# Spacing attention work and gate splits in the last loop of a fused attention and SwiGLU kernel, with a second accumulator bank

## The chip, the core and the metric

The kernel runs on one core of a Trainium2 chip. A core has five engines that run side by side, each with its own in-order stream of instructions: TensorE (matrix products, "PE" in the profile, with its weight loads as "PEld"), VectorE ("DVE"), ScalarE ("ACT"), GpSimd ("POOL") and SyncE ("SP", which here starts DMA transfers). [...]TensorE writes its products into PSUM, a memory of eight banks of 128 partitions by 512 fp32 values. The metric is device time in microseconds, less is better. The kernel before takes 292.16 us, the median of three runs (292.1 to 293.44).

## The reference

Two blocks follow each other. The first is a linear attention on polynomial sketches, the second a SwiGLU layer on its output.

```python
def phi(x):
    a = einsum('rd,bhsd->bhsr', S1, x)          # r = 8
    b = einsum('rd,bhsd->bhsr', S2, x)
    return einsum('bhsi,bhsj->bhsij', a, b).reshape(..., 64)
q_p, k_p = phi(q), phi(k)                       # 4 batches, 4 heads, 1088 tokens, 32 wide
kv  = einsum('bhsf,bhsd->bhfd', k_p, v)
z   = sum(k_p, axis=2)
num = einsum('bhsf,bhfd->bhsd', q_p, kv)
den = einsum('bhsf,bhf->bhs', q_p, z)[..., None] + 1e-06
x   = (num / den) laid out as 4352 tokens x 128
g   = x @ w_gate                                # 128 x 1536
out = (g * sigmoid(g) * (x @ w_val)) @ w_out    # 1536 x 128
```

All inputs and outputs are fp32.

## The kernel before

**Tiling.** The 4352 tokens are cut into twelve blocks, three for each of the four batches, of 384, 384 and 320 tokens. The hidden width of 1536 is twelve chunks of 128. A *unit* `(i, j)` computes chunk `j` of the hidden layer for block `i`: a gate product, a value product, Silu of the gate, and their product, which lands in a slot of `hbuf`. A *down* product (`down`, L962) multiplies one such slot by the rows of `w_out` of that chunk and adds it, in PSUM, to the block's output; after the twelfth, `store` (L993) transposes the accumulator on VectorE (L997) and sends it out. Before the last loop the kernel runs attention for batch 0 and most of the first three blocks' units; the last loop (L1237) runs the other nine blocks, `line`, 108 units counted by `y`, block by block, with attention of batches 2 and 3 threaded through.

**Two forms of a product.** An fp32 product costs TensorE two passes of 384 columns for each weight tile. In `cut_unit` (L887) a product is instead made from parts of its operands: tokens and weights are each split into a high and a low part that TensorE takes in one pass (`x1`, `x0`, `w1`, `wb`) and one correcting combination of both (`xd`, `wd`). Three one-pass products then stand for one fp32 product: `wd` by `xd` (L896), `w1` by `x1` (L904) and `wb` by `x0` (L905). ScalarE evicts the first with a scale (L900), and VectorE adds the sum of the other two to it (L906, the *combine*). `cut_unit` always treats the value product like this. With `both` it treats the gate so too, and the eviction and the combine are twice as wide; without `both` the gate is one fp32 product (L898), and Silu (L912) reads it from PSUM. GpSimd makes the product of gate and value (L917). With `both`, the Silu and the last product of a unit are put off (`ending`) until the next unit has put its first products and its eviction into the streams (`finish`, L927).

**The order of downs.** A unit that is done is appended to `todo`. After every unit of the last loop, up to two downs are taken while more than five are left (L1248), or more than six when the next one would be the first of its block. In that last case a unit passes without a down, and the next takes two.

**PSUM.** Banks are numbered 0 to 7: `g0` = 0, `g1` = 1, `g2` = 2, `acc` = 3, `a` = 4 and 5, `b` = 6 and 7. In the last loop `bank()` hands out the bank whose last hand-out lies furthest back (`used`), leaving out the ones that are held; `pair()` does so among the pairs that start at 0, 4 and 6. Bank 3 is held for the down products of whichever block is under way.

**Attention in the last loop.** `attentions` (L603) is a generator. Each `yield` ends a *part*: a few instructions, mostly VectorE's (a product that makes features, L365, of up to 768 columns; a transpose, L750; the denominator, L735 to L741, five dependent instructions in one part). `parts_of` runs the next part; it stops in front of a yield of `"pe"`, which marks a *group* of TensorE work that is run at the units listed in `GROUPS`. For batch 2 these groups are: kv and the sums (L698), with the sketches of the next keys; the query sketches. For batch 3: the numerators of batch 2 (L758) with kv; the query sketches. The fifth is the numerators of batch 3. After kv, `fold` (L585) and `spread_out` (L711) have VectorE read kv's bank: four short instructions in a row, ending with the transpose at L716. The last of the first three, at L596, makes the third sketch that the query sketches need.

**The order in the streams.** Nothing is reordered by a scheduler: the kernel is written with a manual schedule, and each engine's instructions stand in the order of the Python calls. The order above is thus the order on every engine, and waits follow from data and from banks and buffers that are used again.

The lines of the last loop that matter: L1226 sets `GROUPS` to `(5, 7, 22, 24, 40)` and `GATES` to 18; L1245 uses both products in parts from `GATES` on; L1250 runs one part after every unit up to 21, and after every second from then on.

Of the kernel before, what the change touches and what calls it, by code (L numbers as in the profile page):

```python
# [19 lines left out]
def kernel(  # L20
# [30 lines left out]
    B, H, S, Dh = q.shape  # L51
# [38 lines left out]
    used = {i: 0 for i in range(8)}  # L90
# [4 lines left out]
    def touch(*which):  # L95
        for i in which:
            clock[0] += 1
            used[i] = clock[0]

    def hold(*tags):  # L100
        for t in tags:
            held.update((place[t], place[t] + 1) if t in "ab" else (place[t],))

    def release(*tags):
        for t in tags:
            banks = (place[t], place[t] + 1) if t in "ab" else (place[t],)
            held.difference_update(banks)
            touch(*banks)

    def bank(tag=None):  # L110

        if tag is not None:
            i = place[tag]
        elif oldest[0]:
            i = min((i for i in used if i not in held), key=used.get)
        else:
            i = place[free_banks[turn[0] % len(free_banks)]]
            turn[0] += 1
        touch(i)
        return PS[:, i, :]  # L120
# [7 lines left out]
    def wide(tag):  # L128
        i = place[tag]
        touch(i, i + 1)  # L130
        return PS[:, i : i + 2, :]
# [423 lines left out]
    def turn_keys(b):  # L555

        for c in kpieces:
            turn_k(*c)
            if c[1] == NC and b + 1 < B:
                load_k(b + 1)  # L560
            yield

    def turn_queries(b):

        for x0, x1 in ((0, 4 * kpieces[0][1]), (4 * kpieces[0][1], 4 * NC)):
            nc.vector.transpose(out=qT[:, x0:x1, :], in_=qld[:, x0:x1, :])
            if x1 == 4 * NC and b + 1 < B:
                load_q(b + 1)
            yield
# [33 lines left out]
    def attentions():  # L603

        yield from turn_keys(1)
        yield from turn_queries(1)
        hold("a")
        kp = wide("a")  # L610
        for i, c in enumerate(kpieces):
            key_products(kp[:, i, :], *c)
        ka = apool.tile([P, NC * H, R], FP32, tag="kas", name="kas")

        def sketch(ps, i):
            c0, c1 = kpieces[i]
            return ps[:, i, 0 : 64 * (c1 - c0)].rearrange("p (x t r) -> p x t r", t=2, r=R)

        for i, (c0, c1) in enumerate(kpieces):
            nc.scalar.copy(ka[:, H * c0 : H * c1, :], sketch(kp, i)[:, :, 0, :])  # L620
        phk = apool.tile([P, NC, H, R, R], FP32, tag="phk", name="phk")
        for n, (i, c0, c1) in enumerate(((0, 0, 3), (0, 3, 5), (1, 5, 7), (1, 7, 9))):
            first = H * (c0 - kpieces[i][0])
            kb = sketch(kp, i)[:, first : first + H * (c1 - c0), 1, :]
            key_features(phk, (ka[:, H * c0 : H * c1, :], kb), c0, c1)
            if n == 3:
                release("a")
            if n % 3 != 1:
                yield
        zs, sums = feature_sums(phk)  # L630
        for f in sums:
            f()
        yield from turn_keys(2)
        kvz = wide("a")
        values(kvz[:, 0, :], phk, zs)
        kab, kcopies = sketched(wide("b"), key_products, 2, "kab2")
        fold(kvz[:, 0, :])
        spread = spread_out(1, kvz[:, 0, :])
        hold("a", "b")
        yield  # L640
        qab, copies = sketched(wide("a"), query_sketches, 3, "qab")
        run_copies(copies, 2)
        yield
        run_copies(kcopies, 2)
        release("a", "b")
        for n, _ in enumerate(query_step(1, qab)):
            if n % 2 == 0:
                yield
        yield
        yield  # L650
        numerators(1, spread)
        yield "first"

        phk = apool.tile([P, NC, H, R, R], FP32, tag="phk", name="phk")
        yield from features(phk, kab)
        zs, sums = feature_sums(phk)
        for f in sums:
            f()
        yield from turn_keys(3)
        yield from turn_queries(2)  # L660
        for b in (2, 3):
            yield "pe"
            if b == 3:
                numerators(2, spread)
            hold("a")
            kv = bank()
            release("a")
            values(kv, phk, zs)
            if b == 2:
                kab, copies = sketched(wide("a"), key_products, 2, "kab2")  # L670
                run_copies(copies, 2)
            fold(kv)
            spread = spread_out(b, kv)
            yield
            yield "pe"
            qab, copies = sketched(wide("b"), query_sketches, 3, "qab")
            run_copies(copies, 2)
            yield
            if b == 2:
                yield from turn_queries(3)  # L680
                phk = hbuf[:, NH - 6 :, :].rearrange("p s (n h i j) -> p (s n) h i j", h=1, i=R, j=R)
                phk = phk.rearrange("p (c h) o i j -> p c (h o) i j", h=H)
                yield from features(phk, kab)
                zs, sums = feature_sums(phk)
            yield from beside(query_step(b, qab), sums)
        yield "pe"
        numerators(3, spread)
        yield
# [13 lines left out]
    def values(kv, phk, zs):  # L702

        key_values(kv[:, 0:F], phk, 0, NC)
        for h in range(H):
            nc.tensor.matmul(
                kv[32 * h : 32 * h + 32, F : 2 * F], ones[:], zs[:, F * h : F * h + F],
                start=True, stop=True,
            )

    def spread_out(b, kv):  # L711

        spread = apool.tile([P, H, F], FP32, tag="spread", name="spread")
        nc.vector.transpose(  # L716
            out=spread[:, 0, :].rearrange("p (g d) -> p g d", g=2),
            in_=kv[:, 0:F].rearrange("p (g f) -> p g f", g=2),
        )
        for s in range(1, H):  # L720
            m = P - 32 * s
            nc.sync.dma_start(out=spread[0:m, s, :], in_=spread[P - m : P, 0, :])
            nc.sync.dma_start(out=spread[m:P, s, :], in_=spread[0 : P - m, 0, :])
        if b + 1 < B:
            load_v(b + 1, [nc.sync] * 4)
        return spread
# [64 lines left out]
    acc = {}  # L791
    todo = []
# [134 lines left out]
    def finish():  # L927
        while ending:
            ending.pop(0)()
# [28 lines left out]
    def catch_up():  # L958
        o, sg = lates.pop(0)
        nc.gpsimd.tensor_tensor(out=o, in0=o, in1=sg, op=ALU.mult)  # L960

    def down():  # L962

        i, j = todo.pop(0)
        n = SPLIT if i == LAST else blocks[i][1]
        if j == 0:
            acc[i] = bank("g1" if i == 1 else "acc")
        nc.tensor.matmul(  # L968
            acc[i][:, 0:n],
            wo[:, j, :],  # L970
            hidden[i, j][:, 0:n],
            start=(j == 0),
            stop=(j == NCH - 1),
        )
        if i != LAST:
            hidden.pop((i, j))
            slots.append(slot_of[i, j])
        if j == NCH - 1:
            store(i, n)
# [136 lines left out]
    def parts_of(n):  # L1116

        for _ in range(n):
            if ahead[0] not in ("pe", "end"):
                ahead[0] = next(att, "end")  # L1120
                begun[0] |= ahead[0] == "first"

    def group():
        while ahead[0] != "pe":
            ahead[0] = next(att)
        ahead[0] = next(att, "end")
# [94 lines left out]

    line = [3 * b + k for b in range(1, B) for k in ((0, 2, 1) if b == B - 1 else range(3))]
    END = len(line) * NCH
    GROUPS, GATES = (5, 7, 22, 24, 40), 18  # L1226

    token_steps = {}
    for m, i in enumerate(line[1:], 1):
# [7 lines left out]
    for y in range(END):  # L1237
        i, j = line[y // NCH], y % NCH
        if y in GROUPS:
            group()  # L1240
        if y == END - 1:
            finish()
            unit(i, j)
        else:
            cut_unit(i, j, both=y >= GATES)  # L1245
        for _ in range(2):

            if len(todo) > min(5 + (todo[0][1] == 0), END - y + 1):  # L1248
                down()
        parts_of(y < 22 or y % 2 == 0)  # L1250
        if y == 0:
            gate_rows = cut_weights(wg, lows, nc.vector)
        for n, row in enumerate(gate_rows):
            if y >= (0, 2, 6, 6)[n]:
                take(row, 1)
        for gen in token_steps.get(y, ()):
            next(gen, None)
# [8 lines left out]
    b, x0 = divmod(t0 // 32, NX)  # L1266
# [34 lines left out]
```

## Time and profile before

| what | value |
|---|---|
| median time | 292.16 us |
| profiled span | 290.1 us |
| TensorE busy | 280.2 us, 97% |
| VectorE busy | 207.7 us, 72% |
| ScalarE busy | 173.7 us, 60% |
| GpSimd busy | 161.8 us, 56% |
| last loop starts (y = 0) | 92.6 us |
| combine L906, 384 / 640 / 768 columns | 0.534 / 0.820 / 0.955 us |
| eviction L900, 384 / 640 / 768 columns | 0.490 / 0.704 / 0.811 us |
| feature product L365 of 768 columns, queries | 1.239 us |
| transpose L750 of 768 columns | 0.965 us |
| transpose of an output block L997, 384 / 320 columns | 0.567 / 0.504 us |

How to read it: the page gives for each engine the time in which it executed something, and for each group of instructions a mean time. Matmuls are pipelined: the recorded time of one overlaps that of the next, so an fp32 product, which is recorded as two matmuls of some 0.49 us, is best priced by the distance between starts. The weight loads in front of the products show better where TensorE stood still: the timeline gives, in square brackets, how long the engine was idle before an instruction and what released it. The chain of waits goes back from the last instruction to what each had to wait for; its rows give start, length and work.

### The profile page before, as it was taken

How to read it: one execution, taken by the hardware profiler on the slowest of the kernel's cores; microseconds unless marked ns; L12 is line 12 of the kernel's file. 1: busy time of each engine (PE TensorE's matmuls, PEld its weight loads, DVE VectorE, ACT ScalarE, POOL GpSimd, SP SyncE). 2: the span in 40 equal slices, each digit the busy share in tenths (PEclk: the TensorE clock that was granted, in tenths of full speed). 3: DMA queues.
4: the chain of work that ended last, by engine and by line, in shares of the span. 5: the costliest groups of instructions: out<-in, count | busy, mean ns of one | idle time of the engine just before them, and what ended most of it. 6: DMA issues, size and time to landing. Idle time of an engine off the chain costs nothing.

```text
span 290.1 us, 6038 instructions
## 1 busy us (share of the span) xinstructions
PE 280.2 (97%) x2311; PEld 211.5 (73%) x2311; DVE 207.7 (72%) x337; ACT 173.7 (60%) x347; POOL 161.8 (56%) x183
## 2 busy tenths in 40 slices
PE   7899999999999989989989999999999999999995
PEld 7545566656656857756868878888888988889884
DVE  4997988874677959999489956756656567575741
ACT  3567565732403757545567776677687776777760
POOL 3316322379302984689438655675665666755750
PEclk9999999999999999999999999999999999999999
DMA  6564292302501302000001001001001010010101
GB/s 194 162 208 111 64 311 73 124 32 84 115 15 17 99 17 79 0 14 14 15 3 30 1 2 23 0 0 31 0 0 27 2 24 1 2 27 1 21 4 27
DMA packets 26141, 14.32 MB, mean 49 GB/s; under 512 B 19840, under 2 KB 24192, under 8 KB 26112
## 3 DMA queue, kind: packets, MB, share of 16 engines
q1 hardware_dynamic: 25456, 13.84, 18.3%
q8 instruction: 18, 0.29, 0.4%
q10 hardware_dynamic: 656, 0.10, 0.2%
q14 instruction: 11, 0.09, 0.1%
HBM read 11.41 MB, written 2.23 MB: 47 GB/s over the span
## 4 chain that ended last, share of the span: by engine, by line
PE 86%; DVE 8%; issue 2%; DMA 1%; ACT 1%; SPq 0%; DVEq 0%; ACTq 0%
PE PS L968 27%; PE PS L939 15%; PE PS L904 11%; PE PS L896 11%; PE PS L905 10%; PE PS L898 3%; PE PS L768 2%; PE PS L330 2%; DVE sum L906 1%; DMA kld<-in_k_dram 1%; PE PS L342 1%; PE PS L376 1%; DVE phk L365 1%; PE PS L983 1%; DVE kT L315 1%
## 5 line engine op out<-in xcount | busy, mean ns | idle before, releaser
L917 POOL TENSOR_TENSOR hbuf<-sg,sum 128x384 f32<-128x384 f32 (+1 forms) x107 | 108.9, 1022 | 62.2 <-ACT sg L912 53.4
L906 DVE SCALAR_TENSOR_TENSOR sum<-PS,sum 128x768 f32<-128x768 f32 (+2 forms) x107 | 89.5, 839 | 49.4 <-ACT sum L900 44.6
L900 ACT ACTIVATE sum<-PS 128x768 f32<-128x768 f32 (+2 forms) x107 | 77.2, 721 | 47.0 <-PE PS L896 40.3
L968 PE MATMUL PS<-hbuf,wo 128*128 128x384 f32 (+2 forms) x288 | 103.0, 459 | 0.0
L968 PEld LDWEIGHTS PS<-hbuf,wo 128*128 128x128 f32 x288 | 52.0, 189 | 10.3 <-issue 0.4
L896 PE MATMUL PS<-xd,gphq 128*128 128x384 f32 (+1 forms) x89 | 49.1, 551 | 2.3 <-DVE sum L906 2.3
L912 ACT ACTIVATE sg<-sum 128x384 f32<-128x384 f32 (+1 forms) x89 | 44.0, 495 | 3.5 <-DVE sum L906 3.2
L904 PE MATMUL PS<-x,w 128*128 128x384 f32 (+1 forms) x107 | 40.4, 377 | 0.1
L896 PE MATMUL PS<-xd,wd 128*128 128x384 f32 (+1 forms) x107 | 38.1, 356 | 0.2 <-DVE xd L872 0.2
L905 PE MATMUL PS<-x,wb 128*128 128x384 f32 (+1 forms) x107 | 35.1, 328 | 0.0
L904 PE MATMUL PS<-x,graw 128*128 128x384 f32 (+1 forms) x89 | 29.9, 336 | 0.2 <-ACT xT L785 0.2
L939 PE MATMUL PS<-xT,wg 128*128 128x384 f32 (+1 forms) x74 | 29.5, 480 | 0.0
L939 PE MATMUL PS<-xT,wv 128*128 128x384 f32 (+1 forms) x74 | 28.8, 471 | 0.2 <-DVE wv L276 0.2
L905 PE MATMUL PS<-x,graw 128*128 128x384 f32 (+1 forms) x89 | 29.0, 326 | 0.0
L896 PEld LDWEIGHTS PS<-xd,wd 128*128 128x128 f32 x107 | 20.3, 190 | 10.0 <-issue 0.7
L943 ACT ACTIVATE sg<-PS 128x384 f32<-128x384 f32 (+1 forms) x31 | 14.3, 466 | 21.4 <-PE PS L939 19.8
L896 PEld LDWEIGHTS PS<-xd,gphq 128*128 128x128 f32 x89 | 16.8, 189 | 13.1 <-DVE sum L906 4.9
L954 DVE TENSOR_TENSOR hbuf<-sg,PS 128x384 f32<-128x384 f32 (+1 forms) x31 | 16.2, 524 | 10.5 <-PE PS L939 10.1
L904 PEld LDWEIGHTS PS<-x,w 128*128 128x128 f32 x107 | 20.1, 188 | 2.8 <-DVE sum L906 0.4
L905 PEld LDWEIGHTS PS<-x,wb 128*128 128x128 f32 x107 | 20.1, 188 | 2.4
L939 PEld LDWEIGHTS PS<-xT,wv 128*128 128x128 f32 x74 | 13.8, 190 | 9.2 <-DVE hbuf L954 0.9
L939 PEld LDWEIGHTS PS<-xT,wg 128*128 128x128 f32 x74 | 13.3, 190 | 9.3 <-issue 1.2
(131 smaller groups left out, 346.6 us busy)
## 6 DMA issues: line engine op xcount, KB each, us to landing
kld<-in_k_dram SPq DMA_DIRECT2D x4, 544.0 KB, 3.9
vld<-in_v_dram SPq DMA_DIRECT2D x12, 144.0 KB, 4.6
qld<-in_q_dram SPq DMA_DIRECT2D x3, 544.0 KB, 3.4
raw<-in_moe_w_out_dram SPq DMA_DIRECT2D x4, 384.0 KB, 4.0
out_dram<-o SPq DMA_DIRECT2D x28, 48.0 KB, 1.8
raw<-in_moe_w_gate_dram SPq DMA_DIRECT2D x3, 384.0 KB, 3.2
raw<-in_moe_w_val_dram SPq DMA_DIRECT2D x3, 384.0 KB, 3.5
out_dram<-o SPq DMA_DIRECT2D x16, 40.0 KB, 1.7
```

Source lines behind the costliest of these rows:

```text
L896: nc.tensor.matmul(ds[:, k], wd, xd, start=True, stop=True)
L898: nc.tensor.matmul(g, wg[:, j, :], xT[:, t0 : t0 + n], start=True, stop=True)
L900: nc.scalar.activation(sums, ds, AF.Copy, scale=-1.0 / BETA)
L904: nc.tensor.matmul(ps[:, k], w1, x1, start=True, stop=False)
L905: nc.tensor.matmul(ps[:, k], wb, x0, start=False, stop=True)
L906: nc.vector.scalar_tensor_tensor(out=sums, in0=ps, scalar=1.0 + 1.0 / BETA, in1=sums, op0=ALU.mult, op1=ALU.add)
L912: nc.scalar.activation(sg, sums[:, 0] if both else g, AF.Silu)
L917: nc.gpsimd.tensor_tensor(out=hj[:, 0:n], in0=sg, in1=sums[:, len(ws) - 1], op=ALU.mult)
L939: nc.tensor.matmul(o[:, 0:n], w[:, j, :], xT[:, t0 : t0 + n], start=True, stop=True)
L943: nc.scalar.activation(sg[:, 0:n], g[:, 0:n], AF.Silu)
L954: nc.vector.tensor_tensor(out=hj[:, 0:n], in0=sg[:, 0:n], in1=u[:, 0:n], op=ALU.mult)
L968: nc.tensor.matmul(acc[i][:, 0:n], wo[:, j, :], hidden[i, j][:, 0:n], start=(j == 0), stop=(j == NCH - 1),)
```

## The change

There are four edits, all in the order of work of the last loop and in the choice of banks.

1. *Attention's parts are spaced differently.* One part after every unit up to y = 7, then after two units in three (not those where `y % 3 == 2`), and from y = 26 on after one unit in three. The groups of batch 3 move from 22, 24 and 40 to 26, 28 and 52.
2. *Gates in parts start otherwise.* They were in parts from y = 18 on. Now they are in parts from y = 26 on, and before that in every third unit from y = 11 (11, 14, 17, 20, 23), the ones that have no attention part.
3. *Two accumulator banks in turn.* The third, fifth, seventh and ninth block of the loop collect their downs in bank 2, the others in bank 3; bank 2 is held from y = 26 on. The rule that a down which starts a block waits for one more unit now holds for the second block of the loop only, so for the others each unit keeps its down.
4. *The bank of kv counts as used again* after the VectorE instructions that read it have been put into the stream, so that it isn't the next to be handed out.

The aim of the first two is to keep VectorE's load beside TensorE's even, that of the third to take away the dependence of a block's first down on the transpose of the block before it, and that of the fourth to keep TensorE off a bank that is still being read.

```diff
             kv = bank()
+            kv_bank = [max(used, key=used.get)]
             release("a")
             values(kv, phk, zs)
...
             fold(kv)
             spread = spread_out(b, kv)
+            touch(*kv_bank)
             yield
...
+    line = [3 * b + k for b in range(1, B) for k in ((0, 2, 1) if b == B - 1 else range(3))]
...
         if j == 0:
-            acc[i] = bank("g1" if i == 1 else "acc")
+            acc[i] = bank("g1" if i == 1 else "g2" if i in line[2::2] else "acc")
...
-    line = [3 * b + k for b in range(1, B) for k in ((0, 2, 1) if b == B - 1 else range(3))]
     END = len(line) * NCH
-    GROUPS, GATES = (5, 7, 22, 24, 40), 18
+    GROUPS, GATES = (5, 7, 26, 28, 52), 26
...
         if y in GROUPS:
             group()
+        if y == GATES:
+            hold("g2")
         if y == END - 1:
             finish()
             unit(i, j)
         else:
-            cut_unit(i, j, both=y >= GATES)
+            cut_unit(i, j, both=y >= GATES or (y > 10 and y % 3 == 2))
         for _ in range(2):
 
-            if len(todo) > min(5 + (todo[0][1] == 0), END - y + 1):
+            if len(todo) > min(5 + (todo[0] == (line[1], 0)), END - y + 1):
                 down()
-        parts_of(y < 22 or y % 2 == 0)
+        parts_of(y < 8 or (y % 3 != 2 if y < GATES else y % 3 == 0))
```

## The prediction

> **What bounds the kernel now.** I read the engine shares first, then the windows of each stage, then what the weight loads wait for, and last the timeline around each wait.
>
> ```profile
> PE 280.2 (97%) x2311; PEld 211.5 (73%) x2311; DVE 207.7 (72%) x337; ACT 173.7 (60%) x347; POOL 161.8 (56%) x183
> ...
> PE 86%; DVE 8%; issue 2%; DMA 1%; ACT 1%; SPq 0%; DVEq 0%; ACTq 0%
> ```
>
> TensorE is the bound, but a busy PE hides its waits, so I look at windows:
>
> ```profile
> 109.00:123.00 14.00, 14.00 (x56) 9.88 (x54) 13.64 (x21) 8.80 (x19) 8.37 (x7) 1.00 0.14 40
> 123.00:136.00 13.00, 11.73 (x49) 8.03 (x47) 13.00 (x17) 6.54 (x13) 11.99 (x12) 1.00 0.10 16
> ...
> 176.00:278.00 102.00, 102.00 (x514) 87.01 (x513) 64.52 (x76) 75.20 (x133) 65.12 (x68) 1.00 0.07 12
> ```
>
> The columns are length, then busy time of PE, PEld, DVE, ACT and POOL. From 109 to 136 us VectorE is full (13.64 of 14.00, then 13.00 of 13.00): attention work for batches 2 and 3 beside the combines of L906. From 176 us on it has a third of its time free and TensorE runs without rest. Number the 108 units of the last loop y = 0 to 107: y=6 starts at 102.3, y=15 at 122.0, y=18 at 127.2, y=24 at 144.7, y=44 at 179.1 us. The weight loads' waits, first for 92 to 180, then for 176 to 280 us (total, times, longest):
>
> ```profile
> PEld PS L896 <- DVE sum L906: 5.4, 8, 1.7
> PEld PS L898 <- DVE spread L716: 1.3, 1, 1.3
> ```
>
> ```profile
> PEld PS L904 <- ACT sum L900: 1.4, 6, 0.2
> ```
>
> And in the timeline one example of each:
>
> ```profile
> 103.57 0.30 PEld L898 LDWEIGHTS PS<-xT,wg 128*128 128x128 f32 x2 [1.26 <-DVE spread L716]
> 130.16 0.19 PEld L896 LDWEIGHTS PS<-xd,gphq 128*128 128x128 f32 x1 [1.49 <-DVE sum L906]
> 150.62 0.19 PEld L896 LDWEIGHTS PS<-xd,gphq 128*128 128x128 f32 x1 [1.70 <-DVE sum L906]
> 217.16 0.19 PEld L904 LDWEIGHTS PS<-x,graw 128*128 128x128 f32 x1 [0.23 <-ACT sum L900]
> ```
>
> So there are four kinds of lost time: a gate product put into the bank of kv that VectorE still reads (103.57); VectorE behind at y=15 to 20 (130.16); one long chain of the denominator on VectorE (150.62); and a block boundary, where a unit has no down product to fill the wait for ScalarE (217.16).
>
> Two unit prices come from the chain of waits. With the gate as one fp32 product, from down pair to down pair:
>
> ```profile
> 118.19 0.65 PE PS L968 x2
> ...
> 120.00 0.65 PE PS L968 x2
> ```
>
> 1.81 us. With both products in parts:
>
> ```profile
> 192.49 0.65 PE PS L968 x2
> ...
> 194.19 0.64 PE PS L968 x2
> ```
>
> 1.70 us. Gates in parts save TensorE 0.11 to 0.12 us a unit (about 0.10 at 320 columns), but the combine grows from 0.54 to 0.95 us on VectorE and the eviction L900 from 0.49 to 0.81 us on ScalarE.
>
> **What the Trainium skill says.** *Perfetto Trace Analysis*, section "Identifying the Most-Contended Engine": the matmul busy share is no good measure, weight-load busy is better. The trace agrees: 123 to 136 us shows PE at 90% but weight loads at only 8.03 of 13 us, against 87.01 of 102 later. The same page, "Optimization Strategy": a gap that repeats can mean too few buffers; here it is 0.2 us, six times, once per block, with one accumulator bank. *SBUF — State Buffer*, "SBUF: two separate sides": VectorE with two SBUF inputs and GpSimd take a shared port pair as an exclusive lock. The trace fits: the feature product L365 of 768 takes 0.94 us at 123.98 and 1.68 us at 130.03, with GpSimd busy 11.99 of 13 us. So VectorE's sums below are a little low. *PSUM — Partial Sum Buffer*, "PSUM bank collisions raise a hardware error": banks must be guarded whole; that is why a product waits for any reader of its bank, as at 103.57.
>
> **Part by part.**
>
> *touch(kv_bank) and down threshold (y=5, 6).* In the built order of before, the gate of y=6 goes to bank 0, where kv is, and waits for the last of fold, reduce, s123, spread. After, kv counts as freshly used, that gate goes to bank 4, whose reader (the kab copy) ended at 101.5. One down also moves from y=6 into y=5. The query sketches L330 still need s123, ready at 103.36, and the combine of y=5, at 103.96; TensorE gets to them at about 104.8 to 105.0 in place of 106.06. VectorE stood idle until 109.22 here, so it moves along. **-1.1** (bounds -0.3 and -1.26).
>
> *Parts spread, gates later (y=8 to 25).* I summed VectorE's instructions per unit in the built order, by row means (combine 0.54 or 0.95, feature product 1.25, transpose 0.96, denominator chain 2.7, xd 0.6, o 0.57), against TensorE's 1.81 or 1.70. Before: from y=8 VectorE's arrears grow to 2 us at y=11, 3 at y=13, 4 at y=15, and stay at 3 to 4 until the group at y=22. TensorE's two-unit cushion is about 2 us, so it stalls: y=15 to 20 take 12.37 us for 9.8 us of products, 2.55 us lost. After: three units cost TensorE 2 x 1.81 + 1.70 = 5.3 us, VectorE 2 x 0.54 + 0.95 + two parts of 1.1 = 4.2 us. The sum of arrears starts at 1.4 (y=10), is 0 at y=14 and never over 1.3. The new wait: a unit with both products finishes its Silu only in the next unit, so it has no down behind it, and ScalarE's next evictions queue behind a Silu that waits for VectorE's combine. Following y=17 to 22 through by these durations, TensorE loses 0.1 to 0.3. I leave 0.35 in all. **-2.2** (bounds -2.5 and -0.5).
>
> *Gate count.* Parts before: y=18 to 106, 89 units; after: 11, 14, 17, 20, 23 and 26 to 106, 86 units. Three units more with an fp32 gate at 0.10 to 0.12. **+0.3**, on the path.
>
> *The group of y=22, now 26.* Before, the numerators waited 0.55 + 0.37 us for VectorE and ScalarE in arrears. After, VectorE is level there. **-0.4** (0 to -0.9).
>
> *First gates in parts at 26, and batch 3's denominator.* This chain lies on VectorE thus before:
>
> ```profile
> 146.82 1.04 DVE L735 TENSOR_TENSOR dot<-qab 128x288 f32<-128x288 f32 x1
> 147.90 0.45 DVE L738 TENSOR_REDUCE den<-dot 128x36 f32<-128x288 f32 x1
> 148.39 0.54 DVE L739 TENSOR_SCALAR den<-den 128x36 f32<-128x36 f32 x1
> 148.96 0.38 DVE L740 RECIPROCAL den<-den 128x36 f32<-128x36 f32 x1
> 149.37 0.46 DVE L741 TENSOR_TENSOR qab<-qab,den 128x288 f32<-128x288 f32 x1
> 149.75 1.55 DVE L906 SCALAR_TENSOR_TENSOR sum<-PS,sum 128x640 f32<-128x640 f32 x2
> ```
>
> The combine behind it held TensorE 1.70 us; y=24 to 29 lose 1.2 us net. The change does not break the chain, it only moves it to y=31 and 32, where the downs are 320 wide (0.54 for 0.65), so the cushion is 0.3 us thinner: about 1.5 us again, and 0.2 when the next feature product comes. At y=26 there is no down, and y=27's pair contains kv's bank 1 (fold to spread, about 1 us): 0.4. **+0.6** (0 to +1.3). Later parts, one in three units: 3 x 0.95 + 1.1 = 4.0 of 5.1 us, no stall.
>
> *Two accumulators.* Seven boundaries (y=30, 42, 54, 66, 78, 90, 102): adding each empty unit and the one behind it and subtracting the steady price gives 0.31, 0.15, 0.19, 0.31, 0.15, 0.31, 0.26 us, 1.7 in all. After, the first down of a block follows at once into the other bank, whose transpose ran a block earlier. Bank 2 is not among the pairs, so holding it takes nothing. Only the boundary at y=18 keeps its old form. **-1.6** (-1.2 to -1.7).
>
> Sum: -1.1 - 2.2 + 0.3 - 0.4 + 0.6 - 1.6 = -4.4; 292.16 - 4.4 = 287.8. The small stalls that I can't see lie on one side, so I say **288.0**. All of it reaches the end, because from y=44 TensorE is packed and the tail is the same.
>
> **Rivals.**
> - *The mix loses half.* Each of five units without a down stalls like a boundary, 5 x 0.3 = 1.5, and VectorE's relief is only two thirds (+0.7): 290.2. For it: at y=18, the first both-unit before, much was lost at once. Against: ScalarE's slack there in the mix is 0.6 to 0.8 us.
> - *Only moved.* The denominator chain costs 1.3 more, and the y=15 to 20 stall is replaced by waits on ScalarE, so -2.2 becomes -0.2 and the rest stays: about 291.0 to 291.6. For it: VectorE's total work hardly changes. Against: it is free a third of the time from 176 us on, and that is where one part in three goes.
> - *Slower.* ScalarE is in order: if the Silu of each both-unit holds the two next evictions, each of the five loses 1 us more and nothing of the 2.2 is won: +5 + 0.3 + 0.6 - 1.6 - 1.1 = +3.2, 295.4. Against: the combine of such a unit is done some 2 us before the next both-unit needs ScalarE.
>
> **How the numbers follow.** Forecast 64%, half lost 22%, moved 10%, slower 4%. Faster by over 0.5% means under 290.7: the first two, 86%; within 0.5%: 10%; slower 4%. The range takes the better bounds of parts two and six and of the group (286.8) up to just past the first rival (290.4).
>
> **What would show it.** Right: the wait of L898 for spread gone; 109 to 136 us with weight-load waits on the combine under 0.5 us; the boundary waits for ScalarE gone but for one; a wait of 1.5 us behind the denominator still there, some 10 us later; gate products 21 in place of 18. Wrong: waits of the w1 products for Silu or eviction at y=11, 14, 17, 20, 23, or a longer stall at y=26 to 36 than I allow.

## The result and the profile after

The changed kernel takes 289.4 us (289.35 to 289.75) against 292.13 us before, measured beside it: a ratio of 0.9898, 95% interval 0.987 to 0.9927. The forecast was 288.0, with a range of 286.8 to 290.4. The time lies in the range and the way was right, but 2.7 us were won where 4.1 were forecast, and the experiments show that nearly all of them are the banks'.

The page after, engine shares and the chain by engine; line numbers move on by two to four (L896 is now L898, L906 is L908, L968 is L972):

```profile
PE 278.8 (97%) x2308; PEld 212.1 (74%) x2308; DVE 205.8 (72%) x337; ACT 173.3 (60%) x347; POOL 162.3 (56%) x183
...
PE 88%; DVE 6%; DMA 1%; ACT 1%; issue 1%; SPq 0%; DVEq 0%; ACTq 0%
```

Hardly anything moves here; VectorE's share of the chain fell from 8% to 6%. The same windows as before (length, then PE, PEld, DVE, ACT, POOL):

```profile
109.00:123.00 14.00, 13.57 (x56) 9.84 (x55) 13.24 (x18) 8.71 (x18) 8.96 (x7) 1.00 0.16 42
123.00:136.00 13.00, 13.00 (x55) 9.60 (x53) 11.58 (x19) 8.02 (x17) 12.90 (x11) 1.00 0.10 16
...
176.00:278.00 102.00, 101.75 (x569) 86.75 (x568) 65.69 (x76) 75.04 (x132) 63.64 (x68) 1.00 0.06 10
```

From 123 to 136 us VectorE has room again (11.58 of 13) and weight loads rise from 8.03 to 9.60. But TensorE now stands still a little between 109 and 123, where it did not before. The longer waits of weight loads, from the timeline of the last loop (left out are 0.24 us at 98.75 and 0.55 us at 105.03, which before has too, and 0.27 and 0.25 us behind the denominator, at 162.06 and 171.59):

```profile
114.62 0.19 PEld L898 LDWEIGHTS PS<-xd,gphq 128*128 128x128 f32 x1 [1.05 <-DVE gphq L859]
141.08 1.09 PEld L770 LDWEIGHTS PS<-phT,spread 32*32 32x32 f32 x64 [0.55 <-ACT sg L914]
142.60 1.05 PEld L376 LDWEIGHTS PS<-hbuf,vld 128*32 128x32 f32 x72 [0.43 <-issue]
145.15 0.19 PEld L898 LDWEIGHTS PS<-xd,wd 128*128 128x128 f32 x1 [0.27 <-DVE spread L718]
147.27 1.48 PEld L330 LDWEIGHTS PS<-s,qT 128*32 128x32 f32 x72 [1.10 <-DVE sum L908]
157.77 0.19 PEld L898 LDWEIGHTS PS<-xd,gphq 128*128 128x128 f32 x1 [1.81 <-DVE sum L908]
...
188.73 0.14 PEld L770 LDWEIGHTS PS<-phT,spread 32*32 32x32 f32 x4 [0.55 <-issue]
189.41 1.01 PEld L770 LDWEIGHTS PS<-phT,spread 32*32 32x32 f32 x60 [0.54 <-DVE sum L908]
190.85 0.19 PEld L898 LDWEIGHTS PS<-xd,gphq 128*128 128x128 f32 x1 [0.43 <-issue]
191.71 0.19 PEld L906 LDWEIGHTS PS<-x,graw 128*128 128x128 f32 x1 [0.56 <-ACT xT L787]
```

Gone are the gate's wait for spread at y=6, the waits for the combine at y=15 to 20, and all boundary waits for ScalarE. New are the first line (unit 11), the eighth (the numerators at y=52) and, in its length, the fifth (the query sketches at y=28: 1.10 us, where before waited 0.55). The sixth, behind the denominator, was forecast.

The starts of units in both traces (a unit starts with its first product by `xd`) divide the difference by stage:

| stage | before, us | after, us | difference |
|---|---|---|---|
| start to y=0 | 92.58 | 92.75 | +0.17 |
| y=0 to 6 | 15.10 | 13.90 | -1.20 |
| y=7 to 9 | 5.25 | 5.26 | +0.01 |
| y=10 | 1.81 | 2.71 | +0.90 |
| y=11 to 35 | 49.14 | 47.44 | -1.70 |
| y=36 to 52 | 30.49 | 30.81 | +0.32 |
| y=53 to 105 | 83.84 | 82.84 | -1.00 |
| from y=106 | 11.9 | 11.9 | 0 |

The sum is -2.5, as the spans have it (290.1 and 287.6). The start of y=0 lies ahead of every edit and still moves from one profiled run to the next (92.58 to 94.73 us), so the experiments are compared by the time from y=0 to the end as well: 197.6 us before, 194.9 after.

### The profile page after: what moved, and what is told of

Read it like the earlier page. It is cut to its first block, busy times and chain, and to the rows that moved or that the text cites. A ratio compares the mean times of both kernels' runs of the same rounds, so it can differ in the third digit from the quotient of the medians.

```text
span 287.6 us, 6035 instructions
## 1 busy us (share of the span) xinstructions
PE 278.8 (97%) x2308; PEld 212.1 (74%) x2308; DVE 205.8 (72%) x337; ACT 173.3 (60%) x347; POOL 162.3 (56%) x183
## 4 chain that ended last, share of the span: by engine, by line
PE 88%; DVE 6%; DMA 1%; ACT 1%; issue 1%; SPq 0%; DVEq 0%; ACTq 0%
PE PS L972 26%; PE PS L941 16%; PE PS L898 11%; PE PS L906 10%; PE PS L907 10%; PE PS L900 4%; PE PS L770 2%; PE PS L342 2%; PE PS L330 2%; PE PS L376 2%; DVE sum L908 1%; DMA kld<-in_k_dram 1%; PE PS L987 1%; DVE gphq L859 1%; PE PS L485 1%
## 5 line engine op out<-in xcount | busy, mean ns | idle before, releaser
L919 POOL TENSOR_TENSOR hbuf<-sg,sum 128x384 f32<-128x384 f32 (+1 forms) x107 | 107.6, 1011 | 59.0 <-ACT sg L914 54.7
L908 DVE SCALAR_TENSOR_TENSOR sum<-PS,sum 128x768 f32<-128x768 f32 (+3 forms) x107 | 88.5, 830 | 46.7 <-ACT sum L902 41.0
L972 PE MATMUL PS<-hbuf,wo 128*128 128x384 f32 (+2 forms) x288 | 103.7, 459 | 0.0
L902 ACT ACTIVATE sum<-PS 128x768 f32<-128x768 f32 (+3 forms) x107 | 76.5, 714 | 43.7 <-PE PS L898 40.0
L972 PEld LDWEIGHTS PS<-hbuf,wo 128*128 128x128 f32 x288 | 51.8, 189 | 9.8 <-issue 0.4
L898 PE MATMUL PS<-xd,gphq 128*128 128x384 f32 (+1 forms) x86 | 49.6, 576 | 1.7 <-DVE sum L908 1.3
L914 ACT ACTIVATE sg<-sum 128x384 f32<-128x384 f32 (+1 forms) x86 | 42.4, 493 | 5.5 <-DVE sum L908 5.3
L906 PE MATMUL PS<-x,w 128*128 128x384 f32 (+1 forms) x107 | 41.0, 384 | 0.0
L898 PE MATMUL PS<-xd,wd 128*128 128x384 f32 (+1 forms) x107 | 38.1, 356 | 0.2 <-DVE xd L874 0.2
L906 PE MATMUL PS<-x,graw 128*128 128x384 f32 (+1 forms) x86 | 28.1, 326 | 0.2 <-ACT xT L787 0.2
L898 PEld LDWEIGHTS PS<-xd,wd 128*128 128x128 f32 x107 | 20.3, 190 | 10.5 <-issue 0.7
L907 PE MATMUL PS<-x,graw 128*128 128x384 f32 (+1 forms) x86 | 28.0, 326 | 0.0
L898 PEld LDWEIGHTS PS<-xd,gphq 128*128 128x128 f32 x86 | 16.3, 189 | 12.3 <-DVE sum L908 2.3
L906 PEld LDWEIGHTS PS<-x,w 128*128 128x128 f32 x107 | 20.1, 188 | 2.7
```

The costliest lines, as they stand in the source:

```text
L898: nc.tensor.matmul(ds[:, k], wd, xd, start=True, stop=True)
L902: nc.scalar.activation(sums, ds, AF.Copy, scale=-1.0 / BETA)
L906: nc.tensor.matmul(ps[:, k], w1, x1, start=True, stop=False)
L907: nc.tensor.matmul(ps[:, k], wb, x0, start=False, stop=True)
L908: nc.vector.scalar_tensor_tensor(out=sums, in0=ps, scalar=1.0 + 1.0 / BETA, in1=sums, op0=ALU.mult, op1=ALU.add)
L914: nc.scalar.activation(sg, sums[:, 0] if both else g, AF.Silu)
```

## The experiments

Two theories came out of the traces. A: the spacing of attention and of gates removes VectorE's arrears, but its own new waits give all of that back, so nearly the whole gain is the banks'. B, the prediction's terms: the spacing is worth 1.7 us net and the banks (kv's bank, the accumulators and the rule for downs) 2.7.

**Banks alone, and spacing alone.** The first kernel has the spacing, groups and gates of before and the banks of after; the second the reverse.

```diff
-    GROUPS, GATES = (5, 7, 26, 28, 52), 26
+    GROUPS, GATES = (5, 7, 22, 24, 40), 18
...
-        if y == GATES:
+        if y == 26:
             hold("g2")
...
-            cut_unit(i, j, both=y >= GATES or (y > 10 and y % 3 == 2))
+            cut_unit(i, j, both=y >= GATES)
...
-        parts_of(y < 8 or (y % 3 != 2 if y < GATES else y % 3 == 0))
+        parts_of(y < 22 or y % 2 == 0)
```

> Before's spacing, gates and groups, with the two accumulator banks, the new down rule and the kv bank counted as used. Theory A (from the two traces): banks alone give 1.2 us at y=6 and 1.4 us at the boundaries, and the spacing gives nothing net, so 289.3 to 289.7 us, level with the changed kernel (289.4). Theory B (the prediction's own terms): the spacing is worth 1.7 us net, so this kernel lies that much above the changed one, at 291.1 us.

```diff
-            kv_bank = [max(used, key=used.get)]
...
-            touch(*kv_bank)
...
-            acc[i] = bank("g1" if i == 1 else "g2" if i in line[2::2] else "acc")
+            acc[i] = bank("g1" if i == 1 else "acc")
...
-        if y == GATES:
-            hold("g2")
...
-            if len(todo) > min(5 + (todo[0] == (line[1], 0)), END - y + 1):
+            if len(todo) > min(5 + (todo[0][1] == 0), END - y + 1):
```

> The new spacing, gates and groups, with before's single accumulator bank, down rule and kv bank. Theory A: 2.55 us won at y=15 to 20 are given back at y=10 (0.9), the group of 26 and 28 (0.5), the group of 52 (0.6), the denominator (0.1) and three more fp32 gates (0.3), so 292.0 us, within 0.3 us of before. Theory B: 290.4 us.

Banks alone: 289.99 us, ratio 0.9918 (0.9904 to 0.9931). Spacing alone: 292.07 us, ratio 0.9999 (0.9988 to 1.001). B's 290.4 for the second is excluded, and so is its 291.1 for the first. A holds: by the medians banks alone stand 0.6 us above the changed kernel where A allowed 0.3, but from y=0 to the end its profiled run takes 195.0 us, the changed kernel 194.9: level. Spacing alone takes 197.3 us there, 0.2 less than before. Its timeline shows where its gain went:

```profile
104.09 0.30 PEld L898 LDWEIGHTS PS<-xT,wg 128*128 128x128 f32 x2 [1.25 <-DVE spread L716]
...
116.16 0.19 PEld L896 LDWEIGHTS PS<-xd,gphq 128*128 128x128 f32 x1 [1.06 <-DVE gphq L857]
142.62 1.09 PEld L768 LDWEIGHTS PS<-phT,spread 32*32 32x32 f32 x64 [0.55 <-ACT sg L912]
...
146.69 0.19 PEld L904 LDWEIGHTS PS<-x,w 128*128 128x128 f32 x1 [0.70 <-DVE spread L716]
149.25 1.48 PEld L330 LDWEIGHTS PS<-s,qT 128*32 128x32 f32 x72 [1.08 <-DVE sum L906]
```

Behind 116.16 and up to 142 us no wait is left, where before lost 2.55 us; but there is 1.06 at the start of that stretch, and 0.70 and 1.08 behind it. In the trace of banks alone the old waits stand as they were (total, times, longest, 92 to 180 us):

```profile
PEld PS L898 <- DVE sum L908: 5.6, 9, 1.7
```

**The bank of kv.** The changed kernel without `kv_bank` and `touch`:

```diff
-            kv_bank = [max(used, key=used.get)]
...
-            touch(*kv_bank)
```

> The changed kernel without counting kv's bank as used again. Theory A: the gate of y=6 goes back into kv's bank and waits some 1.3 us for VectorE, nothing absorbs it, 290.6 us. Rival: the wait of the first gate in parts at y=11 for its weight parts absorbs it, 289.5 us, with that wait down from 1.05 us to near 0.

290.46 us, ratio 0.9937 (0.9925 to 0.995): 1.1 us slower than the changed kernel. Its timeline:

```profile
103.81 0.30 PEld L898 LDWEIGHTS PS<-xT,wg 128*128 128x128 f32 x2 [0.75 <-DVE spread L716]
105.64 1.48 PEld L330 LDWEIGHTS PS<-s,qT 128*32 128x32 f32 x72 [0.55 <-ACT sg L912]
115.22 0.19 PEld L896 LDWEIGHTS PS<-xd,gphq 128*128 128x128 f32 x1 [1.05 <-DVE gphq L857]
```

The gate waits for spread again, 0.75 us of it visible since a down now stands in y=5; the later wait stays at 1.05 us and absorbs nothing. Units 5 and 6 take 6.00 us in place of 5.45. The other half of the loss is at y=26, where kv's bank 1 is handed out again in unit 26 and not in unit 27: 0.70 us of wait for spread in place of 0.27, and units 26 and 27 take 5.48 us in place of 5.04.

**One accumulator.** The changed kernel with bank 3 alone and the old rule for a block's first down (the last three hunks of spacing alone).

> The changed kernel with one accumulator bank and the old rule for the first down of a block. Theory A: seven boundaries lose 0.15 to 0.31 us each again, less the 0.07 that three keep, 1.4 us, so 290.8 us. Rival: boundaries hide in other waits, 289.9 us or less.

290.4 us, ratio 0.9934 (0.992 to 0.9948), 1.0 us slower than the changed kernel (0.8 from y=0), between the two expectations. The waits from 150 to 290 us say why it isn't 1.4:

```profile
PEld PS L898 <- DVE sum L908: 1.7, 3, 1.2
PEld PS L906 <- ACT sum L902: 1.6, 7, 0.2
```

All seven boundary waits are back, 1.6 us. But the wait behind the denominator is 1.2 us at the longest, not 1.81. TensorE reaches it some 0.2 us later, having waited at the boundary of y=30 and done two downs in y=31, and VectorE is done 0.36 us sooner, all of it in one short instruction of the denominator (L741, 0.25 us in place of 0.61; the last section has the lines). Units 30 to 35 take 9.93 us here and 10.29 in the changed kernel, so at y=30 the second accumulator won nothing and lost 0.36 us. Units 5 and 6 take 5.44 us, as in the changed kernel: with kv's bank counted as used, the new rule for downs adds nothing there.

**The first gate in parts.**

```diff
-            cut_unit(i, j, both=y >= GATES or (y > 10 and y % 3 == 2))
+            cut_unit(i, j, both=y >= GATES or (y > 13 and y % 3 == 2))
```

> The changed kernel with the gate of y=11 left as one fp32 product: gates in parts in third units from 14. Theory A: the 1.05 us wait at y=11 is for the last weight parts of that very chunk, which VectorE makes in y=8 to 10; without it 0.9 us less and 0.11 us more for the fp32 gate, 288.6 us. Rival: VectorE is in arrears by then and the wait only moves to y=12 to 14, 289.4 us.

288.46 us, ratio 0.9858 (0.9834 to 0.9881): 0.9 us below the changed kernel, and the wait for gphq is gone from the trace without a follower. But the unit starts give this wait only part of the gain: units 10 to 14 take 8.59 us in place of 9.20, 0.6 us less. Another 0.6 us is won at y=27, where the query sketches wait half as long as in the changed kernel (1.10 us):

```profile
146.30 1.48 PEld L330 LDWEIGHTS PS<-s,qT 128*32 128x32 f32 x72 [0.55 <-DVE sum L908]
```

The order in which banks are handed out, followed through the code, explains it: with one gate in parts less, the pairs behind it shift, and unit 27 has its sums in banks 0 and 1, not in 6 and 7, which the sketches fill. So this edit mends two waits, and only the first was meant. VectorE's timeline in the changed kernel shows what the first was:

```profile
111.18 1.36 DVE L874 SCALAR_TENSOR_TENSOR xd<-x,x 128x384 fp32r<-128x384 f32 x1
112.46 0.54 DVE L908 SCALAR_TENSOR_TENSOR sum<-PS,sum 128x384 f32<-128x384 f32 x1
112.93 0.69 DVE L566 STREAM_TRANSPOSE qT<-qld 128x512 f32<-128x512 f32 x1
113.55 1.01 DVE L859 SCALAR_TENSOR_TENSOR gphq<-hbuf,graw 128x384 fp32r<-128x384 f32 x1
```

The last weight parts of chunks 9 to 11 are ready at 114.56; unit 11 is the first that reads them, and reads them as the very first operand.

**The unit of the last numerators.**

```diff
-    GROUPS, GATES = (5, 7, 26, 28, 52), 26
+    GROUPS, GATES = (5, 7, 26, 28, 53), 26
```

> The changed kernel with the last group (numerators of batch 3) at 53 in place of 52. Theory A: at 52 the unit ahead has its sums in banks 6 and 7, which the numerators fill too, so they wait 0.54 us for its combine; at 53 the unit ahead has them in 0 and 1: 0.5 us less, 288.9 us, and that wait gone. Rival: the numerators wait for their operands or for the eviction whatever the bank, 289.4 us.

289.1 us, ratio 0.9887 (0.986 to 0.9915). The times alone can't tell 0.3 us from nothing. The trace can (176 to 280 us):

```profile
PEld PS L906 <- ACT xT L787: 0.6, 1, 0.6
PEld PS L770 <- ACT sum L902: 0.5, 1, 0.5
PEld PS L898 <- issue: 0.4, 1, 0.4
```

The numerators' wait for the combine is gone, the 0.5 us in front of their first weight load stays, and from y=0 to the end it takes 194.3 us in place of 194.9.

**The unit of the query sketches.**

```diff
-    GROUPS, GATES = (5, 7, 26, 28, 52), 26
+    GROUPS, GATES = (5, 7, 26, 29, 52), 26
```

> The changed kernel with the query sketches of batch 3 at 29 in place of 28. Theory A: at 28 the unit ahead has its sums in banks 6 and 7, where the sketches go, and they wait 1.10 us for its combine, of which 0.55 us is there at the other sketches too; at 29 it is 0.55 us, so 288.9 us. Rival: the denominator follows the later sketches more closely and takes it back, 289.4 us.

289.34 us, ratio 0.99 (0.987 to 0.9929): the times alone leave it open. In the trace the wait is halved and the one behind the denominator no longer than it was:

```profile
148.46 1.48 PEld L330 LDWEIGHTS PS<-s,qT 128*32 128x32 f32 x72 [0.55 <-issue]
157.44 0.19 PEld L898 LDWEIGHTS PS<-xd,gphq 128*128 128x128 f32 x1 [1.82 <-DVE sum L908]
```

The denominator still starts at y=30; from y=0 to the end it takes 194.4 us in place of 194.9, as A expected.

**The denominator in two parts.**

```diff
         nc.vector.tensor_reduce(out=den[:], in_=dot[:], axis=AX.X, op=ALU.add)
+        if b == 3:
+            yield
...
-        parts_of(y < 8 or (y % 3 != 2 if y < GATES else y % 3 == 0))
+        parts_of(y < 8 or (y % 3 != 2 if y < GATES else y % 3 == 0 or y == 31))
```

> The changed kernel with the denominator of batch 3 in two parts, two instructions after y=30 and three after y=31. Theory A: TensorE's 1.81 us wait comes from 2.7 us of VectorE work in one piece; in two pieces of 1.2 and 1.6 us TensorE's cushion of about 2 us takes most of it, 1.2 us less, 288.2 us. Rival: what counts is VectorE's sum over y=30 to 36, which is the same, so 289.1 us or more and the wait appears later.

288.61 us, ratio 0.9871 (0.9846 to 0.9897), 0.8 us below the changed kernel and nearer to A than to its rival. The 1.81 us have become two short waits (and the 0.27 us behind them 0.42); units 30 to 35 take 9.19 us in place of 10.29:

```profile
158.19 0.19 PEld L900 LDWEIGHTS PS<-xd,gphq 128*128 128x128 f32 x1 [0.25 <-DVE sum L910]
159.92 0.19 PEld L900 LDWEIGHTS PS<-xd,gphq 128*128 128x128 f32 x1 [0.56 <-DVE sum L910]
```

**All four together, with two and with three parts of the denominator.** `GROUPS` is then `(5, 7, 26, 29, 53)`, gates in parts start at 14. The second kernel has one more split; beyond the first, which it keeps, its edit against the changed kernel is:

```diff
         nc.vector.reciprocal(den[:], den[:])
+        if b == 3:
+            yield
...
-        parts_of(y < 8 or (y % 3 != 2 if y < GATES else y % 3 == 0))
+        parts_of(y < 8 or (y % 3 != 2 if y < GATES else y % 3 == 0 or y in (31, 32)))
```

> The changed kernel with all four mendings: first gate in parts at 14, query sketches of batch 3 at 29, last numerators at 53, the denominator of batch 3 in two parts. Theory A (four separate waits in a row on a packed TensorE): the separate gains add, 0.9 + 0.3 + 0.3 + 0.8, so 287.0 to 287.3 us. Rival (they share one slack of VectorE): not under 288.0 us.

> The same with the denominator in three parts (after y=30, 31, 32). If the remaining waits behind it come from the longer second piece (1.6 us beside a combine of 0.8), 0.3 to 0.5 us less than with two parts; if from VectorE's sum over y=30 to 36, no change within 0.1 us.

287.49 us, ratio 0.9828 (0.9804 to 0.9852), and 287.12 us, ratio 0.9817 (0.9795 to 0.9839). The first lies 0.2 us above A's band and well below the rival's 288.0, but A's reason for the number does not hold: the four gains do not add. From y=0 to the end the four kernels won 1.2, 0.5, 0.6 and 1.1 us, 3.4 in all; together they win 2.3, which is what the first gate and the split denominator win by themselves. The sketches were mended already by the move of the first gate: units 26 to 29 take 7.27 us, with the first gate's edit alone 7.29. And the numerators wait again:

```profile
188.98 1.01 PEld L772 LDWEIGHTS PS<-phT,spread 32*32 32x32 f32 x60 [0.54 <-DVE sum L910]
```

By the order of hand-outs the unit ahead of them, y=52, now has its sums in banks 6 and 7; units 51 to 53 take 7.93 us, as in the changed kernel, where the last group's edit alone took 7.30. Each edit had shifted the banks for all that follows.

The third part of the denominator lowers the median by 0.4 us, but the single runs of the two kernels overlap and from y=0 the traces differ by 0.2 us only: the wait of 0.55 us at 156.94 is gone, and one of 0.39 us stands behind it in its place. Neither expectation for it is confirmed. This has the lowest median: 1.8% below before, 0.8% below the change.

**The mended spacing on the old banks.** The four mendings, two parts of the denominator, and the last three hunks and the kv bank of spacing alone.

> The new spacing with those four mendings, but with before's single accumulator, down rule and kv bank. Theory A: spacing is worth 2.5 us at y=15 to 20 and loses it in waits of its own, so with these mended it comes to 292.1 - 2.3 = 289.8 us, against 292.07 for the spacing as it was. Rival: the spacing wins nothing of its own and the mendings don't reach it, 291 us or more.

289.66 us, ratio 0.9899 (0.988 to 0.9918), by 2.4 us better than the spacing as it was. Of these, 0.7 us come from the split denominator (units 30 to 35 take 9.18 us in place of 9.92), whose wait before has as well. So with its own waits at the first gate, at kv's bank and at the sketches taken away the spacing wins 1.7 us more, some 1.9 in all against before; the numerators wait here as they did.

## Why the prediction was right, and where not

The time lay in the range, but the sum behind it did not hold, and that the range held is in part luck: it reaches up to 290.4 because of a rival, in which units without a down stall, and that did not happen. The terms of the banks, -1.1 and -1.6, were right. The terms of the spacing, -1.7 together, came to 0.2 us or less. By terms:

- *kv's bank:* forecast -1.1; measured -1.20 at y=0 to 6. Right, and the bank was the reason: with the old rule for downs it is all still there (5.44 us for units 5 and 6, against 6.66 before), and the new rule alone, with kv's bank not counted as used, brings half (6.00).
- *Arrears of VectorE at y=15 to 20:* forecast -2.2. The unit starts give 5.3 us for each three units from y=12 to 23, which is the bare price of the products: all 2.55 us are won there. The feared hold-up of ScalarE in units without a down did not come. What failed is what stands ahead of it: "The sum of arrears starts at 1.4 (y=10)" (in the same breath with "never over 1.3") was read as harmless because the combine has two units of cushion. The weight split at the end of these arrears has none, since unit 11 reads it first. Unit 10 takes 0.9 us longer for it; with that gate left as one product, units 10 to 14 take 0.6 us less.
- *Three more fp32 gates:* +0.3 forecast, on the path. No run has this term by itself; three times the difference of the two unit prices (1.81 and 1.70) is 0.3.
- *The group of 22, now 26, and the first gates in parts behind it:* forecast -0.4, and 0.4 within the next term. The waits at both groups of batch 3 sum to 1.90 us before and to 2.35 after, some 0.5 more. VectorE was level, as said, but I didn't ask in which banks the unit ahead of each group has its sums: at y=27 they are 6 and 7, where the sketches go. Wrong in sign, small in size.
- *The denominator:* forecast 1.5 us, measured 1.81 at the wait, 7 us later than before; right in kind. That narrower downs make the cushion thinner was not tested, and is not the whole reason: with one accumulator the downs are as narrow and the wait is 1.21. That the second accumulator's gain at y=30 would be used up here was not foreseen.
- *The numerators of batch 3:* priced at nothing, measured +0.6. The same slip: banks 6 and 7.
- *Two accumulators:* forecast -1.6. With banks alone the units at the seven boundaries and behind them take 1.5 us less; about 0.06 us stays at some (y=66 takes 1.48 us, 1.42 is steady). Right, but undoing them in the changed kernel costs 0.8 to 1.0 us only, because of the denominator.

Against the unrounded sum of -4.4 the measured -2.7 is 1.7 us less. The three waits that were not foreseen, for an operand at its first use or for a bank at a group, stand against it with 0.9, 0.6 and 0.5 us. The surprise is in the parts: an edit that won 2.5 us where it aimed gave nearly all of it back elsewhere.

One word on the price of a gate: an fp32 product was introduced as two passes. The trace does record two matmuls for it, but they take 0.65 us from start to start, and one-pass products of the same width start 0.17 us apart (before, in a unit with both products in parts):

```profile
193.33 0.34 PE L904 MATMUL PS<-x,graw 128*128 128x384 f32 x1
193.50 0.34 PE L905 MATMUL PS<-x,graw 128*128 128x384 f32 x1
193.68 0.34 PE L904 MATMUL PS<-x,w 128*128 128x384 f32 x1
193.85 0.34 PE L905 MATMUL PS<-x,wb 128*128 128x384 f32 x1
```

Three of these take 0.52 us, so the parts save 0.12 us a product; by a count of passes they would have lost.

## What to carry to other kernels

When work is moved off a full engine, find for every product that now comes sooner which operand it reads first and when that is made, and for every block of work on fixed banks which banks the unit ahead has just filled: three such waits, with the denominator's and the dearer gates, ate a gain of 2.5 us. Each wait could be mended by moving one index, but where banks are handed out in turn such a move also shifts the banks of everything behind it: one edit here mended a second wait unasked, and two that helped alone did nothing together with the rest. So look at the banks again after every move. A long run of dependent short instructions on an in-order engine held TensorE for 1.81 us; cut in two, it cost 1.1 us less.

## What was not expected of the hardware

In every trace here the first weight load of the query sketches in the last loop came at least 0.55 us after the load ahead of it, and that of the value sums (L376) behind the numerators 0.43 us, whatever was named as the cause; mending the waits never brought them lower. Why is open.

Some of VectorE's instructions stretched with what GpSimd did in the same time. The combination that makes `xd` took 1.36 us at 111.18 us after, and 0.54 us at 113.31 us before. In the first case it began while GpSimd was at a product, and ended 0.42 us after it; in the second GpSimd stood still. GpSimd's line for after comes first, then VectorE's and GpSimd's for before:

```profile
110.93 1.19 POOL L919 TENSOR_TENSOR hbuf<-sg,sum 128x384 f32<-128x384 f32 x1 [1.02 <-DVE sum L908]
```

```profile
113.31 0.54 DVE L872 SCALAR_TENSOR_TENSOR xd<-x,x 128x384 fp32r<-128x384 f32 x1
```

```profile
111.96 1.01 POOL L917 TENSOR_TENSOR hbuf<-sg,sum 128x384 f32<-128x384 f32 x1 [1.02 <-DVE sum L906]
114.46 1.58 POOL L917 TENSOR_TENSOR hbuf<-sg,sum 128x384 f32<-128x384 f32 x1 [1.49 <-DVE sum L906]
```

The denominator's addition of 1e-6 (L741) is the same instruction in the changed kernel and with one accumulator. Here is the changed kernel, VectorE and then GpSimd:

```profile
155.47 0.61 DVE L741 TENSOR_SCALAR den<-den 128x36 f32<-128x36 f32 x1
```

```profile
155.17 0.88 POOL L919 TENSOR_TENSOR hbuf<-sg,sum 128x320 f32<-128x320 f32 x1 [0.53 <-ACT sg L914]
```

And with one accumulator:

```profile
155.82 0.25 DVE L741 TENSOR_SCALAR den<-den 128x36 f32<-128x36 f32 x1
```

```profile
154.10 1.93 POOL L919 TENSOR_TENSOR hbuf<-sg,sum 128x320 f32<-128x320 f32 x2 [0.66 <-ACT sg L914]
```

Both times it ends 0.03 to 0.04 us after GpSimd's product does, at 156.08 and at 156.07 us. Counted from y=0 the denominator starts at the same time in both runs, and GpSimd's product ends 0.37 us sooner with one accumulator: that is the 0.36 us. No experiment moved GpSimd's products alone, so that they hold VectorE is read from the traces.
